# Block products of a two-level fast multiplication: the two whole ones also by quarters, one operand's sums streamed, another order

## The chip, the core and the metric

The kernel runs on one core of one Trainium2 chip. Time is device microseconds of one execution; it took 1370.39 us, the median of three (1369.78 to 1371.06). A core has TensorE (PE in the profile; PEld is its weight load), VectorE (DVE), ScalarE (ACT), GpSimd (POOL) and SyncE (SP), which here only issues DMAs. TensorE writes to PSUM, which holds eight banks of 512 float32 per partition; everything else lies in SBUF, 128 partitions wide.

## The reference, cut to what matters

```python
# q, k, v: (8, 8, 576, 64); tau = 0.02
scores = (1 / sqrt(64)) * (q @ k^T)
scores = where(scores >= max(scores) - tau, scores, -1e9)
attn   = exp(scores - max) / sum
x      = (attn @ v)  reshaped to (4608, 512)
g      = x @ w_gate                 # (512, 1536)
val    = x @ w_val                  # (512, 1536)
out    = (g * sigmoid(g) * val) @ w_out     # (1536, 512)
```

All of it is float32.

## The kernel before

**The work.** The eight batches are chunks 0 to 7 of 512 tokens; the last 64 tokens of each batch are gathered into a ninth, chunk 8 (`B` in the code). For every chunk the gate and value products are formed in six groups (`Group`, later `LateGroup`), and then the output product with w_out, which is what the change rewrites. The output product has an activation matrix of 512 tokens by 1536 and a weight matrix of 1536 by 512. From chunk 2 on (`DEEP = 2`) it is done in two levels of a seven-product scheme (Strassen's in Winograd's form). At the first level each matrix is cut into four blocks, and four blocks and three or four sums of blocks give seven pairs; a pair's product is called a step here. At the second level a step's two operands are cut in quarters again, so that the step itself is seven quarter products.

**The steps of a chunk** are methods of `Deep` (line 1433 on): p1 (operand 0), p2 (1), p3 (2), p4 (3), p5 (4), p6 (5), p7 (6). Steps by quarters call `nested` (line 1499): seven times three matmuls of 128x128 by 128x128, their matmul at line 1510. Steps p5 and p3 are whole: `flat` (line 1524) runs 2 x 6 matmuls with 256 columns, line 1519, with the tile name py. A nested step wants inner sums of its activation operand (`inner_sums`, line 1483: s3, s1, s2, s4, four additions of 128x384) and three sums of its weight operand. The weight sums are made once, on POOL during chunk 2, by `deepen` (line 1416): t1, t2, t4 go to a place in SBUF and t3 replaces a quarter of the operand. Five operands are treated so (`NESTED = 0, 1, 5, 6, 3`). A nested result is seven quarter products in two PSUM banks, and `combine` (line 1535) adds them up to an output block by four additions.

**Sums across steps.** p1's result is copied by ACT to SBUF (`copies`, line 1530), p2 is added in PSUM on top of it, combined and shipped; the copy is put back into PSUM by ACT (line 1625) so that p6 can be accumulated on it. p6's sum is copied out again, combined, and p3 on p5 is added; p7 is accumulated on the same bank and copied out, and p4 comes last on the same bank. `corner` (line 1681) adds p5's copy to the combined block.

**What sets the order.** The order of instructions is found when the program is built, by a planner (`Plan`, line 28): work on DVE, ACT, POOL and SP is given to it as jobs with an estimated duration, what they wait for and a rank (0 first), and it places them in time beside TensorE, whose order is written out. At run time each engine goes through its list in this order, waiting on semaphores. While attention of batches 1 to 7 runs (`halved`, 28 head pairs with three score groups each, line 1770), the feed-forward work of the earlier chunk is drawn from `sequence` (line 2007) between the score groups, so many steps a group as the tables say (`EARLY`, `SECOND`, `THIRD`, `MAIN`). `POOLED`, `EXCHANGE` and `CUTS` say for each score group how many of its tiles POOL scales and which engines exchange maxima and form thresholds. `attend` (line 1888, matmul xa at line 1904) multiplies the finished probabilities, which DVE has transposed (line 1883), with v.

**The tail.** After the last attend `tail[0]` is true, and chunks 7 and 8 run with nothing between their steps; the sums, which POOL does before, are then DVE's. A chunk's order of steps is

```python
# chunks 2 to 6
p1_first, last_gates, p1_rest, p2, p5, p6, p3, p7, p4
# chunk 7                     # chunk 8
p1, gates_end, p2, p7_alone,  p1, gates_end, p2, p7_alone,
p5, p6_alone, p3, p4_alone    p5_end, p6_alone, p4_alone, p3_end
```

**Weights of the next groups.** `flow` has two slots of seven 512-column parts for the gate and value weights. `load_flow` (line 949) loads a slot in two DMAs (1 MB and 0.75 MB). During the output steps the slots also hold activation sums (`s2`, `s3`, `place`), so a load is issued only after the step that reads these (`next_flow`, line 1731).

## Time and profile before

| what | us |
|---|---|
| median of three executions (1369.78 to 1371.06) | 1370.39 |
| the profiled execution | 1370.31 |
| its span in the profile | 1368.2 |
| DVE / ACT / POOL busy | 1090.6 / 866.7 / 714.2 |
| period of a middle chunk (p1_rest at 519.8, 666.4, 813.2, 959.8, 1106.5) | 146.6 |

Line numbers (L1510) are those of the kernel before; a group of instructions is named by line, engine, operation and out<-in tiles. A matmul of float32 leaves two records, so counts on TensorE are twice the number of matmuls. A timeline line gives start, duration, engine, line, operation and shape; what stands in brackets is how long the engine had been idle before it, and who ended that. The granted clock of TensorE was 0.997 of full speed.

### The profile page before, as it was taken

The numbers are of one execution on the slowest core, as the hardware profiler recorded it, in microseconds if no ns is written. First come the engines' busy times: TensorE is split into PE (matmuls) and PEld (weight loads), VectorE is DVE, ScalarE is ACT, GpSimd is POOL, SyncE is SP. The second block draws the span as 40 slices with busy tenths as digits, with TensorE's granted clock in tenths as the row PEclk, the third lists the DMA queues.
The fourth block names the chain that finished last, engine by engine and source line by source line (L and its number), as shares of the span: only waits on it lengthen the run. The fifth ranks groups of instructions, "written<-read, shape, count | busy, mean of one in ns | idle before, by whom it ended". The sixth has DMA issues, their size and how long they took to land.

```text
span 1368.2 us, 39123 instructions
## 1 busy us (share of the span) xinstructions
PE 1348.9 (99%) x15590; PEld 1126.1 (82%) x15590; DVE 1090.6 (80%) x2860; ACT 866.7 (63%) x2218; POOL 714.2 (52%) x664
## 2 busy tenths in 40 slices
PE   9999999999999999999999999999999999999998
PEld 7777887777788788878887788888887788999888
DVE  6788998888877778887878877887888776797786
ACT  6788765767765767677767676677767674330330
POOL 2688698754655669434972487437843592000000
PEclk9999999999999999999999999999999999999999
DMA  8752414466425440654154514543255404423411
GB/s 173 184 204 71 102 37 137 115 184 174 120 52 157 135 105 27 193 153 113 37 171 129 160 25 135 157 142 68 69 161 145 111 27 155 150 78 139 162 54 32
DMA packets 208293, 162.31 MB, mean 119 GB/s; under 512 B 166128, under 2 KB 180464, under 8 KB 202736
## 3 DMA queue, kind: packets, MB, share of 16 engines
q1 hardware_dynamic: 203920, 158.86, 41.2%
q8 instruction: 123, 2.02, 0.6%
q10 hardware_dynamic: 4192, 0.95, 0.3%
q14 instruction: 58, 0.48, 0.1%
HBM read 138.28 MB, written 21.50 MB: 117 GB/s over the span
## 4 chain that ended last, share of the span: by engine, by line
PE 89%; DVE 4%; POOL 2%; DMA 1%; issue 1%; SPq 1%; ACT 1%; ACTq 0%; DVEq 0%; POOLq 0%
PE pb L1021 17%; PE pa L1021 12%; PE px L1510 12%; PE sc L1770 10%; PE pe L1021 9%; PE xa L1904 9%; PE po L1303 5%; PE py L1519 5%; PE pg L1234 1%; PE sc L1188 1%; PE pv L1234 1%; PE pe L1188 1%; PE sc L1021 1%; POOL pall L495 1%; SPq L391 1%
## 5 line engine op out<-in xcount | busy, mean ns | idle before, releaser
L1846 ACT ACTIVATE pall<-sc,nm 128x288 f32<-128x288 f32 x504 | 234.2, 500 | 78.2 <-DVE pall L1848 42.5
L1848 DVE SCALAR_TENSOR_TENSOR pall<-sc,th,pall 128x288 f32<-128x288 f32 x504 | 243.7, 513 | 38.4 <-ACT pall L1846 21.9
L1021 PE MATMUL pb<-xall,big 128*128 128x256 f32 x1104 | 262.0, 380 | 0.0
L1021 PEld LDWEIGHTS pb<-xall,big 128*128 128x128 f32 x1104 | 207.5, 190 | 29.6 <-issue 1.6
L1883 DVE STREAM_TRANSPOSE pall<-pall 128x576 f32<-128x576 f32 x252 | 188.1, 764 | 28.9 <-POOL pall L1878 15.5
L1881 ACT ACTIVATE pall<-pall,ri 128x288 f32<-128x288 f32 x416 | 190.5, 526 | 22.8 <-DVE ri L1869 22.0
L1021 PE MATMUL pa<-xall,big 128*128 128x256 f32 x752 | 178.9, 381 | 0.3 <-ACT sc L1028 0.3
L1021 PEld LDWEIGHTS pa<-xall,big 128*128 128x128 f32 x752 | 140.7, 190 | 20.9 <-issue 2.5
L872 POOL TENSOR_TENSOR hall<-hall,tmp 128x512 f32<-128x512 f32 x80 | 102.5, 1281 | 104.9 <-DVE hall L1080 64.3
L1770 PE MATMUL sc<-kT,qT 64*32 64x288 f32 (+1 forms) x5376 | 145.5, 345 | 0.1
L1805 DVE TENSOR_REDUCE mx<-sc 128x2 f32<-128x576 f32 x168 | 118.4, 746 | 34.0 <-PE sc L1770 33.1
L1878 POOL TENSOR_SCALAR pall<-pall,ri 128x288 f32<-128x288 f32 x88 | 87.9, 1006 | 104.4 <-DVE ri L1869 75.4
L1021 PE MATMUL pe<-xall,big 128*128 128x256 f32 x576 | 138.4, 383 | 0.9 <-ACT pall L1881 0.9
L1770 PEld LDWEIGHTS sc<-kT,qT 64*32 64x32 f32 x5376 | 98.2, 106 | 49.9 <-issue 10.6
L1904 PE MATMUL xa<-pall,vall 64*32 64x288 f32 x4032 | 129.6, 404 | 3.0 <-PE px L1510 2.7
L1021 PEld LDWEIGHTS pe<-xall,big 128*128 128x128 f32 x576 | 107.6, 190 | 19.7 <-issue 4.3
L1904 PEld LDWEIGHTS xa<-pall,vall 64*32 64x32 f32 x4032 | 83.3, 107 | 42.0 <-issue 5.0
L872 POOL TENSOR_TENSOR tmp<-tmp 128x512 f32<-128x512 f32 x36 | 45.8, 1273 | 84.9 <-ACT tmp L1102 84.9
L1863 ACT COPY sums<-sums 32x6 f32<-32x6 f32 x336 | 66.6, 198 | 28.0 <-DVE pall L1848 23.9
L1079 ACT ACTIVATE vall<-tmp 128x512 f32<-128x512 f32 x96 | 60.0, 628 | 34.0 <-DVE tmp L1092 27.2
L1519 PE MATMUL py<-wo,hall 128*128 128x256 f32 x336 | 74.8, 379 | 0.0
L872 POOL TENSOR_TENSOR hall<-hall 128x384 f32<-128x384 f32 (+2 forms) x67 | 67.4, 1018 | 8.9 <-PE px L1510 8.2
(272 smaller groups left out, 2509.2 us busy)
## 6 DMA issues: line engine op xcount, KB each, us to landing
big<-sums_hbm SPq DMA_DIRECT2D x42, 1024.0 KB, 5.2
big<-sums_hbm SPq DMA_DIRECT2D x48, 768.0 KB, 4.6
vall<-in_v_dram SPq DMA_DIRECT2D x112, 144.0 KB, 3.1
out_dram<-big SPq DMA_DIRECT2D x32, 256.0 KB, 3.1
qT<-in_q_dram SPq DMA_DIRECT2D x112, 72.0 KB, 4.7
kT<-in_k_dram SPq DMA_DIRECT2D x112, 72.0 KB, 3.0
wo<-in_moe_w_gate_dram SPq DMA_DIRECT2D x16, 384.0 KB, 3.8
wo<-in_moe_w_val_dram SPq DMA_DIRECT2D x16, 384.0 KB, 4.7
```

The costliest lines, as they stand in the source:

```text
L872: return lambda: nc.gpsimd.tensor_tensor(out=out, in0=a, in1=b, op=op)
L1021: nc.tensor.matmul(ps[:, i], w[:, k_, i * P:(i + 1) * P], x[:, k_, :], start=first and i == k_ == 0, stop=True, skip_group_check=True)
L1510: nc.tensor.matmul(ps, a[:, f, :], ws[n][:, f, :], start=bank_ not in begun, stop=True, skip_group_check=True)
L1519: nc.tensor.matmul(ps(), a[:, f, i * P:(i + 1) * P], operands[o][:, f, :], start=first and f == 0, stop=True, skip_group_check=True)
L1770: nc.tensor.matmul(to[g * G:(g + 1) * G], qT[hs, col:col + G], kT[hs, c * SH + lo:c * SH + hi], start=True, stop=True)
L1805: rs.append(job("DVE", 0.72 if w > 1 else 0.42, lambda h=h: nc.vector.tensor_reduce(out=mx[:, n0 + h:n1 + h + 1:max(2, n1 - n0), 0], in_=s ...
L1846: ej = job("ACT", 0.44, lambda x=x, n=n: nc.scalar.activation(ps[x], scs[x], AF.Exp, bias=nm[:, n:n + 1]), ej, rank=top, on=on[x])
L1848: masks[x] = job("DVE", 0.48, lambda x=x, n=n: nc.vector.scalar_tensor_tensor(out=ps[x], in0=scs[x], scalar=th[:, n:n + 1], in1=ps[x], op0 ...
L1878: scaled.append(job("POOL", 1.02, lambda x=x, n=n: nc.gpsimd.tensor_scalar(out=x, in0=x, scalar1=ri[:, n:n + 1], scalar2=None, op0=ALU.mul ...
L1881: scaled.append(job("ACT", 0.46, lambda x=x, n=n: nc.scalar.activation(x, x, AF.Copy, scale=ri[:, n:n + 1]), rj, rank=rank))
L1883: seg["turned"].append(job("DVE", 0.72, lambda both=both: nc.vector.transpose(out=both, in_=both), *scaled, rank=rank))
L1904: nc.tensor.matmul(holds[a].ap()[x * G:(x + 1) * G, 0:SH].rearrange("d (i q) -> d i q", q=G), vr[rs, h, j, ds], p[rs, h, :, j, :], start=( ...
```

## The change

- Steps p5 and p3 become nested steps like the others, except the very last product, p3 of chunk 8 (`p3_end`), which stays whole. `flat` and `p5_end` go; `flat_half` stays for `p3_end`.
- Operands 4 and 2 get weight sums too, so seven are deepened. Those of operand 4 lie in spare places of SBUF. Those of operand 2 are stored in DRAM (`deep_hbm`) and loaded in each chunk to places that are free just then (`fetch_streamed`, two DMAs of 0.4 and 0.2 MB). Since p3 of chunk 8 reads the operand itself, the quarter that t3 replaced is saved too and loaded again after chunk 7 (`restore`).
- `inner_sums(4)` is added behind p1 and `inner_sums(2)` behind p7; each is four additions of 128x384. In the tail the inner sums of operands 2 and 3 are POOL's.
- The order of the steps is p7, p2, p5, p6, p4, p3 after p1 (in chunk 6 p3 before p4; in the tail p7, p2, p6, p5, p4, p3). p7 and p5 get pairs of banks of their own. p7's copy and p6's bank are added by DVE, and ACT copies this sum back to PSUM for p4 to be accumulated on. `corner` adds p5's copy to that sum (896 columns) and then combines.
- `next_flow` calls move: slot 0's second part behind p7, slot 0's first behind p6, slot 1's second behind p5, and slot 1's first behind p3 (behind p6 before).
- `s_place` moves to `pall`, and the tables of steps, pooled scales, exchanges and cuts have other values.

```diff
@@ -1406,5 +1406,17 @@
+    SPARE_SUMS, STREAMED = 4, 2
+    loose = whole[:, SPARE + P + NF2 * TC:SPARE + P + NF2 * TC + 2 * QW]
+    ends = vends.rearrange("p a n -> p (a n)")[:, 0:QW]
+    streamed = tmp.rearrange("p a f n -> p (a f n)")[:, 2 * NQ * P:2 * NQ * P + 2 * QW], flow[:, GW + 3 * HW:GW + 3 * HW + QW]
+    deep_stored = []
     def deeper_part(o, n):
-        lo = (3 * NESTED.index(o) + n) * QW
-        return deeper[:, lo:lo + QW].rearrange("p (f q) -> p f q", q=P)
+        if o in (SPARE_SUMS, STREAMED):
+            two, one = (loose, ends) if o == SPARE_SUMS else streamed
+            place = two[:, n * QW:(n + 1) * QW] if n < 2 else one
+        else:
+            lo = (3 * NESTED.index(o) + n) * QW
+            place = deeper[:, lo:lo + QW]
+        return place.rearrange("p (f q) -> p f q", q=P)
@@ -1417,3 +1429,4 @@
         b11, b12, b21, b22 = quarters(operands[o])
-        t1, t2, t4 = (deeper_part(o, n) for n in range(3))
+        t1, t2, t4 = (deeper_part(o, n) if o != STREAMED else free_place[:, n * QW:(n + 1) * QW].rearrange("p (f q) -> p f q", q=P)
+                      for n in range(3))
         j = job("POOL", 1.0, pool_tt(t1, b12, b11, ALU.subtract), *deps, rank=3)
@@ -1421,3 +1434,23 @@
         j = job("POOL", 1.0, pool_tt(t4, b21, t2, ALU.subtract), j, rank=3)
-        deep_jobs[o] = [job("POOL", 1.0, pool_tt(b12, b22, b12, ALU.subtract), j, rank=3)]
+        kept = None
+        if o == STREAMED:
+            deep_stored.append(job("SP", 0.1, lambda: nc.sync.dma_start(out=deep_hbm[:, 0:3 * QW], in_=free_place[:, 0:3 * QW]), j, lag=2.0, moves=2.2))
+            kept = job("SP", 0.3, lambda: nc.sync.dma_start(out=deep_hbm[:, 3 * QW:].rearrange("p (f q) -> p f q", q=P), in_=b12), *deps,
+                       lag=2.0, moves=0.8)
+            deep_stored.append(kept)
+        deep_jobs[o] = [job("POOL", 1.0, pool_tt(b12, b22, b12, ALU.subtract), j, kept, rank=3)]
+    def fetch_streamed(*deps):
+        two, one = streamed
+        def fn():
+            nc.sync.dma_start(out=two, in_=deep_hbm[:, 0:2 * QW])
+            nc.sync.dma_start(out=one, in_=deep_hbm[:, 2 * QW:3 * QW])
+        return job("SP", 0.2, fn, *deep_stored, *deps, lag=1.6, moves=2.2)
+    def restore(*deps):
+        b12 = quarters(operands[STREAMED])[1]
+        deep_jobs[STREAMED] = [job("SP", 0.3, lambda: nc.sync.dma_start(
+            out=b12, in_=deep_hbm[:, 3 * QW:].rearrange("p (f q) -> p f q", q=P)), *deps, lag=2.0, moves=0.8)]
...
@@ -1436,3 +1469,3 @@
         def __init__(self, c, mark):
-            self.c = c
+            self.c, self.at_end = c, tail[0]
             halves = [hall[:, t].rearrange("p g f n -> p (g f) n") for t in range(2)]
@@ -1442,2 +1475,3 @@
             self.place = flow[:, 0:KW]
+            self.late_place = flow[:, GW + 4 * HW:GW + 4 * HW + KW]
             assert GW - KW >= 4 * HW
@@ -1446,10 +1480,13 @@
             self.blocks = 0
+            self.c5 = self.u2 = None
             if tail[0]:
-                self.steps = deque([self.p1, self.gates_end, self.p2, self.p7_alone, self.p5, self.p6_alone, self.p3, self.p4_alone])
-                self.spaces = [pall[:, n * CW:(n + 1) * CW] for n in range(5)]
+                self.steps = deque([self.p1, self.gates_end, self.p7_alone, self.p2, self.p6_alone, self.p5, self.p4_alone, self.p3])
+                self.spaces = [*(pall[:, n * CW:(n + 1) * CW] for n in range(4)), w_second[:, 0:CW]]
                 if c == B:
-                    self.steps = deque([self.p1, self.gates_end, self.p2, self.p7_alone, self.p5_end, self.p6_alone, self.p4_alone, self.p3_end])
+                    self.steps = deque([self.p1, self.gates_end, self.p7_alone, self.p2, self.p6_alone, self.p5, self.p4_alone, self.p3_end])
             else:
-                self.steps = deque([self.p1_first, self.last_gates, self.p1_rest, self.p2, self.p5, self.p6, self.p3, self.p7, self.p4])
-                self.spaces = [*spaces, None, spaces[1]]
+                self.steps = deque([self.p1_first, self.last_gates, self.p1_rest, self.p7, self.p2, self.p5, self.p6, self.p4, self.p3])
+                if c == B - 2:
+                    self.steps = deque([self.p1_first, self.last_gates, self.p1_rest, self.p7, self.p2, self.p5, self.p6, self.p3, self.p4])
+                self.spaces = [*spaces, None, spaces[0]]
             self.ready["a11"] = [gated[c, 0, x] for x in range(NF2 // 2)]
@@ -1462,3 +1499,3 @@
             self.ready["s1"] = [self.sum(self.a21, self.a21, self.a22, ALU.add, x, j3[x], gated[c, 1, n + x]) for x in range(n - 1)]
-            self.inner_sums(6, self.s3, free_place, j3)
+            self.inner_sums(6, self.s3, free_place, j3, *deep_stored)
@@ -1476,2 +1513,5 @@
             self.inner_sums(5, self.s2, self.place, self.ready["s2"], self.m1)
+            self.inner_sums(4, self.a21, self.late_place, self.ready["s1"], mark)
+            if self.c < B:
+                self.fetched = fetch_streamed(*u_list[3].jobs, *s_list[0].jobs, mark)
@@ -1487,4 +1527,4 @@
             s1, s2, s3, s4 = (flat[:, n * QW:(n + 1) * QW].rearrange("p (f q) -> p f q", q=P) for n in range(4))
-            tt, eng, took = (dve_tt, "DVE", 0.49) if tail[0] else (pool_tt, "POOL", 1.0)
-            rank = 1 if o in (1, 5) else 2
+            tt, eng, took = (dve_tt, "DVE", 0.49) if self.at_end and o not in (2, 3) else (pool_tt, "POOL", 1.0)
+            rank = 1 if o in ((1, 4, 5) if self.at_end else (1, 4, 5)) else 2
             j3 = job(eng, took, tt(s3, a11, a21, ALU.subtract), *ready, *deps, rank=rank)
...
@@ -1628,18 +1662,22 @@
             self.ready["s4"] = s4
+            if self.c == B - 2:
+                self.last_sums(self.m7)
             self.inner_sums(3, self.a22, self.a11, self.ready["a22"], m)
+            if self.c < B and self.c != B - 2:
+                self.last_sums(self.m7)
         def p5(self):
-            self.y = y = take("py")
-            m = self.flat(4, self.a21, y, True, *y.deps, *self.ready["s1"])
-            t = self.spaces[4]
-            self.c5 = job("ACT", 0.57, lambda: nc.scalar.copy(t[:, 0:DM], y.ap()), m, *u_list[1].jobs, *u_list[2].jobs, *u_list[3].jobs, rank=0)
...
+            self.y, deps = self.pair("py")
+            m = self.nested(4, self.y, True, *deps)
+            self.c5 = self.copies(self.spaces[4], self.y, m, *(() if self.at_end else self.z))
+            self.next_flow(1, 1, m)
+            if not self.at_end:
+                self.try_corner()
+                return
+            t, j = self.spaces, self.u3
+            if self.c == B:
+                self.done(self.y, *self.c5)
+                j = job("DVE", 1.05, dve_tt(t[2], t[2], t[4], ALU.add), j, *self.c5, rank=1)
+                self.n12, self.j12 = self.combine(t[2], j)
+            self.corner(t[3], j)
@@ -1647,4 +1685,5 @@
             o = self.block(self.n12).rearrange("p (i n) -> p i n", i=2)
-            for i, y in enumerate(self.ys):
-                m = self.flat_half(2, self.a12, i, lambda y=y: y.ap()[:, 0:DM2], False, self.c5[i], *self.ready["s4"])
+            for i in range(2):
+                y = take("py")
+                m = self.flat_half(2, self.a12, i, lambda y=y: y.ap()[:, 0:DM2], True, *y.deps, *self.ready["s4"], *deep_jobs[2])
                 j = job("DVE", 0.4, lambda i=i, y=y: nc.vector.tensor_tensor(out=o[:, i], in0=y.ap()[:, 0:DM2], in1=o[:, i], op=ALU.add),
@@ -1657,30 +1696,47 @@
             m = self.nested(5, self.x, False, *self.z)
+            x, t = self.x, self.spaces
             self.next_flow(0, 0, m)
-            self.next_flow(1, 0, m, *self.ready["s4"])
-            self.c6 = self.copies(self.spaces[2], self.x, m, *n_list[0].jobs, *n_list[1].jobs)
-            self.n12, self.j12 = self.combine(self.spaces[2], *self.c6)
+            self.c6 = self.copies(t[2], x, m, *n_list[0].jobs, *n_list[1].jobs)
+            a, b = x
+            js = [job("DVE", 0.7, lambda: nc.vector.tensor_tensor(out=t[1][:, 0:4 * P], in0=a.ap(), in1=t[1][:, 0:4 * P], op=ALU.add),
+                      m, *self.c7, rank=0),
+                  job("DVE", 0.56, lambda: nc.vector.tensor_tensor(out=t[1][:, 4 * P:CW], in0=b.ap()[:, 0:3 * P], in1=t[1][:, 4 * P:CW],
+                                                                   op=ALU.add), m, *self.c7, rank=0)]
+            self.u2 = js[1]
+            self.try_corner()
+            self.z2 = [job("ACT", 0.57, lambda: nc.scalar.copy(a.ap(), t[1][:, 0:4 * P]), js[0], self.c6[0], rank=0),
+                       job("ACT", 0.46, lambda: nc.scalar.copy(b.ap()[:, 0:3 * P], t[1][:, 4 * P:CW]), js[1], self.c6[1], rank=0)]
         def p3(self):
-            y = self.y
-            m = self.flat(2, self.a12, y, False, self.c5, *self.ready["s4"])
-            o = self.block(self.n12)
-            j = job("DVE", 0.7, lambda: nc.vector.tensor_tensor(out=o, in0=y.ap(), in1=o, op=ALU.add), m, self.j12, rank=0)
-            y.read_by(j)
-            y.done(True)
-            self.ship(0, 1, self.n12, j)
+            t = self.spaces[2]
+            m = self.nested(2, self.y, False, *self.c5, self.fetched)
+            n, j = self.combine(t, *self.add(t, self.y, t, m, *self.c6, self.u3 if self.at_end else None))
+            self.ship(0, 1, n, j)
             for b in n_list:
                 b.jobs = [*b.jobs, j]
-            self.next_flow(1, 1, m)
+            for b in (u_list[3], s_list[0]):
+                b.jobs = [*b.jobs, m]
+            self.next_flow(1, 0, m)
+            if self.at_end:
+                restore(m)
         def p7(self):
-            m = self.nested(6, self.x, False, *self.c6)
-            self.next_flow(0, 1, m)
-            self.c7 = self.copies(self.spaces[0], self.x, m, *self.z)
-            self.corner(self.spaces[0], *self.c7)
+            y, deps = self.pair("py")
+            m = self.nested(6, y, True, *deps)
+            self.next_flow(0, 1, m, *self.ready["s2"])
+            self.c7 = self.copies(self.spaces[1], y, m, *u_list[1].jobs, *u_list[2].jobs, *u_list[3].jobs)
+            self.done(y, *self.c7)
+            self.m7 = m
+        def try_corner(self):
+            if self.c5 and self.u2:
+                self.corner(self.spaces[1], self.u2)
+        def last_sums(self, *deps):
+            self.inner_sums(2, self.a12, free_place, self.ready["s4"], *deps)
         def corner(self, t, *deps):
-            n, j = self.combine(t, *deps)
-            o, s = self.block(n), self.spaces[4][:, 0:DM]
-            tt, eng, took = (dve_tt, "DVE", 0.62) if tail[0] else (pool_tt, "POOL", 1.3)
-            j = job(eng, took, tt(o, o, s, ALU.add), j, *(self.c5 if self.c == B else [self.c5]), rank=1)
+            s = self.spaces[4]
+            tt, eng, took = (dve_tt, "DVE", 1.05) if tail[0] else (pool_tt, "POOL", 2.1)
+            n, j = self.combine(s, job(eng, took, tt(s, s, t, ALU.add), *deps, *self.c5, rank=1))
             self.ship(1, 1, n, j)
@@ -1688,5 +1744,7 @@
                 b.jobs = [*b.jobs, j]
+            if self.at_end:
+                w_users[1] = [j]
         def p4(self):
-            m = self.nested(3, self.x, False, *self.c7)
+            m = self.nested(3, self.x, False, *self.z2)
             n, j = self.combine(self.x, m, psum=True)
@@ -1708,7 +1766,4 @@
             self.next_flow(0, 0, m)
-            self.next_flow(1, 0, m, *self.ready["s4"])
             self.next_flow(0, 1, self.m7)
-            self.n12, self.j12 = self.combine(t[2], *self.c6)
-            self.u3 = job("DVE", 1.05, dve_tt(t[3], t[2], t[3], ALU.add), *self.c6, *self.c7, rank=1)
-            self.corner(t[3], self.u3)
+            self.u3 = j = job("DVE", 1.05, dve_tt(t[3], t[2], t[3], ALU.add), *self.c6, *self.c7, rank=1)
@@ -2032,10 +2087,10 @@
     EARLY = (2, 2, 3, 1, 2, 3, 1, 3, 4, 1, 3, 3)
-    SECOND = (2, 5, 7, 3, 6, 5, 3, 6, 5, 3, 4, 4)
-    THIRD = (2, 5, 8, 3, 5, 7, 4, 7, 7, 1, 2, 2)
-    MAIN = (1, 3, 8, 3, 5, 7, 4, 7, 7, 1, 2, 2)
-    LATE = (0, 1, 4)
-    LATE_SECOND = (0, 2, 4)
-    POOLED = (2, 1, 1, 0, 2, 1, 1, 0, 0, 0, 1, 1)
-    EXCHANGE = ('BOTH', 'DVE', 'BOTH', 'ACT', 'BOTH', 'DVE', 'DVE', 'ACT', 'ACT', 'BOTH', 'ACT', 'BOTH')
-    CUTS = ('ACT', 'DVE', 'ACT', 'DVE', 'DVE', 'ACT', 'ACT', 'DVE', 'DVE', 'DVE', 'ACT', 'DVE')
+    SECOND = (2, 5, 7, 3, 6, 5, 3, 6, 5, 5, 3, 5)
+    THIRD = (2, 5, 6, 5, 5, 7, 2, 7, 4, 4, 2, 2)
+    MAIN = (2, 4, 6, 3, 6, 7, 3, 7, 7, 1, 2, 2)
+    LATE = (2, 3, 4)
+    LATE_SECOND = (1, 2, 3, 4)
+    POOLED = (1, 3, 0, 2, 1, 1, 0, 0, 0, 0, 0, 0)
+    EXCHANGE = ('ACT', 'BOTH', 'ACT', 'ACT', 'DVE', 'DVE', 'ACT', 'DVE', 'DVE', 'BOTH', 'BOTH', 'BOTH')
+    CUTS = ('DVE', 'DVE', 'ACT', 'DVE', 'ACT', 'DVE', 'DVE', 'ACT', 'DVE', 'DVE', 'DVE', 'DVE')
```

31 lines of the change are left out of this document (11 added, 20 removed).

## The prediction

> **What bounds the kernel now.** I read the share of each engine first, then the chain of work that ended last, the waits of TensorE, and then the timelines of the stretches that the change rewrites.
>
> ```profile
> span 1368.2 us, 39123 instructions
> ## 1 busy us (share of the span) xinstructions
> PE 1348.9 (99%) x15590; PEld 1126.1 (82%) x15590; DVE 1090.6 (80%) x2860; ACT 866.7 (63%) x2218; POOL 714.2 (52%) x664
> ```
>
> TensorE is busy for 99% of the span, and the waits that its view of waits lists come to 15 us, 9 of them in the first attention stage (lines 265 to 531). So the time is TensorE's own work, plus whatever new waits the change makes. The chain in the output stage of chunk 3 (one of seven two-level chunks, 2 to 8; the middle ones repeat every 146.6 us), columns start, duration, what:
>
> ```profile
> 666.41 3.56 PE px L1510 x30
> 669.97 0.53 issue
> 670.49 4.70 PE xa L1904 x144
> 675.19 1.47 PE sc L1770 x58
> 676.66 4.88 PE px L1510 x42
> 681.54 5.18 PE py L1519 x24
> 686.72 1.65 PE sc L1770 x64
> 688.37 4.88 PE px L1510 x42
> 693.25 5.18 PE py L1519 x24
> ```
>
> A px piece of 42 records is one block product by quarters (7 x 3 matmuls of 128 columns, two records each); a py piece of 24 is one whole product (12 matmuls of 256 columns). After a score group (sc) the px piece takes 4.88. In the tail, with no scores between, the two stand side by side:
>
> ```profile
> 1237.54 5.18 PE py L1519 x24
> 1242.72 4.69 PE px L1510 x42
> ```
>
> **Removed: TensorE work.** Steps p5 and p3 (operands 4 and 2) of chunks 2 to 8 are the 14 whole products; 13 become quarter products (the last one of chunk 8 stays whole). The instruction order confirms it: 156 fewer 128x256 and 273 more 128x128 matmuls. Each saves 5.18 - 4.69 = 0.49 us: 13 x 0.49 = **-6.4 us**, on the path. The number of score and attend runs stays 85, so the 0.19 of a first piece after scores is not changed. The Trainium skill (TensorE: Matmul & The Clock Gate, section "Wait — 56ns, not 53.3ns?") puts a fixed 2.5 ns on every matmul beside its columns; from its figures, with two passes a record, a record of this quarter product is an estimated 109 ns and the saving 7.7 us; a record of the whole product comes out at 216 ns, as in the trace (5.18/24). The rows give 4.69/42 = 112 ns, and the sum goes by them.
>
> **Moved: the order of softmax work.** Five times attend waits half a microsecond:
>
> ```profile
> PE xa L1904 <- PE px L1510: 2.7, 5, 0.5
> ```
>
> The real releaser is DVE's last transpose of the probabilities, since attend depends on it and it ends at 670.39 just before attend starts at 670.49:
>
> ```profile
> 666.47 1.42 DVE L1805 TENSOR_REDUCE mx<-sc 128x2 f32<-128x576 f32 x2 [0.18 <-PE sc L1770]
> ...
> 669.61 0.78 DVE L1883 STREAM_TRANSPOSE pall<-pall 128x576 f32<-128x576 f32 x1
> ```
>
> In chunks 3 to 6 the new tables put that transpose and the last gate product ahead of the score maxima. ACT's last scaled tile (666.85) then lets it end near 667.9, two microseconds before attend can start. The gain lies between 0 (the delayed maxima make the next score group late instead) and 5 x 0.53 = 2.7; I take 4 x 0.53 = **-2.1 us**.
>
> **Added: waits at p4.** The old order put p3 or an attend between a copy and the product that reads it. Now p6 is followed in chunks 2 to 5 by one score group (1.65) and then by p4, which needs ACT's new copies of the summed block back to PSUM. Behind p6's end ACT has 0.17 to start, 0.58 + 0.48 for the old pair of copies (rows at 693.35 and 694.43 show 0.59 and 0.47) and 0.58 for the first new one: 1.8, and 0.1 to reach TensorE. That is 1.9 against 1.65: 0.25 late. DVE's two new PSUM additions (0.69 and 0.55, as in the tail) run beside it.
>
> The other input of p4 is POOL's. POOL's order in such a chunk runs without a gap from the last gate product to the last inner sum of p4: 8 sums of 128x512 at 1.24 pitch, 19 of 128x384 at 1.0, 4 token sums at 0.72, one query scaling at 1.7, and the new 128x896 addition at 1.28 x 896/512 = 2.2. Sum 35.7 us. The 384 price is from
>
> ```profile
> L872 POOL TENSOR_TENSOR hall<-hall 128x384 f32<-128x384 f32 x40 | 39.7, 1001 | 8.9 <-PE px L1510 8.2
> ```
>
> If the gate product starts at 667.25 (last gates end 664.76; the DVE product now at 666.5 for 0.69), POOL is done at 702.95. TensorE reaches p4 at 669.97 + 6.17 + 4.88 + 4.69 + 1.65 + 4.88 + 4.69 + 1.65 = 698.6 and needs that sum for its last seventh, 0.19 + 4.0 later, at 702.8, plus the 0.25 above. So the two meet within 0.2. I cost 0.4 a chunk, 4 x 0.4 = **+1.6 us**, between 0.25 (1.0) and 2.1 a chunk (8.4, below). In chunk 6 p3 stands ahead of p4 and an attend between them; nothing is charged.
>
> **Added: the tail of chunk 7.** In the tail all sums were DVE's, and POOL was idle from 1139.5 on. Now the inner sums of p4 and p3 go to POOL, 8 operations in chunk 7 and 4 in chunk 8. The only place in this trace where DVE operations with two SBUF inputs meet POOL is the weight stage:
>
> ```profile
> 89.82 0.94 DVE L348 SCALAR_TENSOR_TENSOR big<-wo,big 128x768 uint32<-128x768 uint32 x1
> 96.71 2.88 DVE L348 SCALAR_TENSOR_TENSOR big<-wo,big 128x768 uint32<-128x768 uint32 x2
> ```
>
> ```profile
> 96.64 1.27 POOL L611 TENSOR_TENSOR hall<-hall,tmp 128x512 f32<-128x512 f32 x1
> ```
>
> Two of 0.94 took 2.88 while POOL held 96.64 to 97.91: DVE stood for 1.0 until POOL had ended. By this row the sums exclude each other. In chunk 7, in old times, p2 now ends at 1237.55 and p6 follows. POOL starts the four inner sums of p4 there. DVE adds four PSUM pieces until 1239.7 and has six SBUF sums left, two of which p6 needs for its last two sevenths. Alternating with POOL's third and fourth sum (1.0 each), those two land at 1243.05 and 1244.4; p6 asks for them at 1240.9 and one seventh later: 2.25 + 0.65 = **+2.9 us**. Without exclusion they land at 1241.0 and 1242.3, which costs 0.8. I take 2.9. Chunk 8 has no such meeting: without eight token sums, DVE is done with p6's inputs before p2 ends.
>
> The Trainium skill (SBUF — State Buffer, section "SBUF: two separate sides") calls the port pair that DVE and GpSimd share an exclusive lock for the whole instruction. It speaks against this move, and the row agrees; that float32 sums do the same is shown by no row of before.
>
> **At nothing.** The streamed operand: two loads (0.4 and 0.2 MB) per chunk, issued behind p1, read by p3 some 30 us later, against 5.2 us for a 1 MB load; if that cover goes, p3 waits for the rest. The first half of the next chunk's second weight slot is now loaded after p3 instead of p6, some 18 us before its reader in the middle chunks and 10 in the tail (against 5.2); queued behind it on SP are only loads with later readers. Eight more POOL operations build the two new operands in chunk 2, where POOL has gaps of 3 to 7 us. For small waits of scheduling that I do not see, **-0.1 to +1**, taken as 0. The last store still leaves after the last whole product, so the 3.7 us behind TensorE stay.
>
> Sum: -6.4 - 2.1 + 1.6 + 2.9 = -4.0. The profiled execution took 1370.31 us (span 1368.2 and 2.1 around it), 0.08 under the median 1370.39, so the forecast is **1366.3 us**.
>
> **Rivals.**
> - The saving is eaten (24%): attend's wait stays or moves to the next score group, and p4 waits 1.0 a chunk: -6.4 + 4.0 + 2.9 = +0.5, 1370.8. For it: DVE's maxima really move back by 1.4 us. Against: the score group reuses banks that are freed in turn.
> - POOL becomes the bound at p4 (13%, slower): one chain of 35.7 us without slack, four times. If the gate product starts at 668.8 as it did before (1.6 late) and chained sums take 1.03 (4.13 for four in the old timeline, 0.5 over 16 of them), p4 waits 2.1: 8.4 instead of 1.6, and attend's gain goes with it, since the same late DVE causes both: -6.4 + 8.4 + 2.9 = +4.9, 1375.2. It makes the kernel slower than can be overlooked once p4 waits 1.6 a chunk.
> - It goes better (18%): no exclusion in the tail and all of attend's wait gone: -6.4 - 2.7 + 1.2 + 0.8 = -7.1, 1363.2.
> - That the products are not replaced is excluded by the instruction order.
>
> **Chances and range.** The forecast, 1364 to 1367.6, has 45%. A measurement of this kernel can tell about 0.2%, 2.7 us. Faster by more: 45 + 18 = 63%; within it 24%; slower 13%. The range leaves out most of the slower rival and the end of the better one: 1362.5 to 1371.8. The likeliest side's own range is 1362.5 to 1367.6.
>
> **What would show it.** One py piece of 24 records is left, all other products are pieces of 42 at 4.7 to 4.9; attend's five waits vanish; the waits of TensorE of the px products in chunks 2 to 5 name ACT or POOL at p4 and stay under half a microsecond; in chunk 7 p6 shows a DVE wait of two to three, with DVE sums of 0.5 stretched to 1.5 beside POOL. Wrong would be p4 waits above 1.5, a wait of p3 for the streamed load, or new waits at the score groups.

## The result: slower, and where the time appears

The changed kernel takes 1409.81 us, the median of five (1405.56 to 1412.54), beside 1371.06 of the kernel before (five, 1369.78 to 1373.25): a ratio of 1.0274, 95% interval 1.0248 to 1.0301. The forecast was 1366.3. The profiled execution took 1405.66.

The first lines of its page; the columns are as in the page of before:

```profile
span 1403.9 us, 39744 instructions
...
PE 1359.2 (97%) x15824; PEld 1134.6 (81%) x15824; DVE 1135.2 (81%) x2896; ACT 879.9 (63%) x2224; POOL 770.2 (55%) x715
```

TensorE is busy 10.3 us longer, though its products became shorter, and idle for the rest of the 35.7 by which the span grew. Its waits (total, times, longest):

```profile
PE sc L1825 <- DVE pall L1903: 11.5, 5, 4.8
PE sc L1825 <- DMA qT<-in_q_dram: 5.7, 1, 5.7
...
PE xa L1959 <- issue: 4.3, 1, 4.3
...
PE px L1550 <- DVE big L876: 1.9, 2, 1.6
...
PE px L1550 <- ACT px L1707: 0.7, 1, 0.7
PE xa L1959 <- PE px L1550: 0.7, 1, 0.7
```

The score groups (sc) wait for VectorE's masks (line 1903, 1848 before), which they did not do before; new waits there are one of the signs of being wrong that the prediction names. The 5.7 put down to a DMA has the same cause: masks stand ahead of the last query transpose in VectorE's list. Attend's wait of five halves of a microsecond is down to one, as forecast. VectorE's list behind the first of these waits (start, duration), in chunk 2:

```profile
549.69 0.12 DVE L1891 TENSOR_REDUCE nm<-mx 128x6 f32<-128x12 f32 x1
549.85 6.71 DVE L1895 TENSOR_SCALAR th<-nm,cut 128x6 f32<-128x6 f32 x1
556.48 0.77 DVE L1938 STREAM_TRANSPOSE pall<-pall 128x576 f32<-128x576 f32 x1
```

The threshold, six numbers a partition, takes 6.71 us; the median of its 62 is 0.36. In the kernel before none of the thresholds takes over 1.02 (duration ns min/median/max):

```profile
L1840 DVE TENSOR_SCALAR th<-nm,cut x52: 221/241/1019, 150.0 to 1132.0; 128x6 f32<-128x6 f32 x52
```

GpSimd at the time of the 6.71:

```profile
548.05 3.72 POOL L873 TENSOR_TENSOR hall<-hall,big 128x512 f32<-128x512 f32 x3
551.72 1.01 POOL L873 TENSOR_TENSOR hall<-hall 128x384 f32<-128x384 f32 x1
...
555.53 1.00 POOL L873 TENSOR_TENSOR hall<-hall 128x384 f32<-128x384 f32 x1
```

Its last sum ends at 556.53, and the threshold at 556.56. The same happens in chunks 4, 5 and 6 (6.95, 6.93 and 7.13 us, each ending 0.03 behind GpSimd's run), not in chunk 3 (1.21). By the times between attends, chunks 2, 4 and 5 are 153 to 156 us long and chunk 3 is 147; chunk 6 has no such time, since attention ends in it. Four pauses of TensorE of 4.3 to 5.7 us follow (at 561, 863, 1018 and 1179). In the four stretches of 50 us that hold them TensorE's granted clock is 0.93, in the four ahead of these 1.00. Two of them (bounds; length; busy PE, PEld, DVE, ACT, POOL with their instructions; clock, DMA share, GB/s):

```profile
800.00:850.00 50.00, 50.00 (x650) 42.57 (x642) 40.46 (x116) 37.13 (x95) 42.53 (x41) 1.00 0.25 64
850.00:900.00 50.00, 44.98 (x559) 37.84 (x558) 41.45 (x97) 29.49 (x81) 29.37 (x31) 0.93 0.45 128
```

The score group that follows the pause of 4.8 us, at 863.21, takes 3.57 where others take 1.72.

### The profile page after: what moved, and what is told of

It is laid out like the page before. It is cut to its first block, busy times and chain, and to the rows that moved or that the text cites. A ratio compares the mean times of both kernels' runs of the same rounds, so it can differ in the third digit from the quotient of the medians.

```text
span 1403.9 us, 39744 instructions
## 1 busy us (share of the span) xinstructions
PE 1359.2 (97%) x15824; PEld 1134.6 (81%) x15824; DVE 1135.2 (81%) x2896; ACT 879.9 (63%) x2224; POOL 770.2 (55%) x715
## 4 chain that ended last, share of the span: by engine, by line
PE 82%; DVE 9%; DMA 2%; issue 2%; POOL 2%; ACT 2%; SPq 1%; DVEq 0%; ACTq 0%; POOLq 0%
PE pb L1022 18%; PE pa L1022 12%; PE sc L1825 9%; PE xa L1959 9%; PE pe L1022 9%; PE px L1550 8%; PE po L1303 5%; PE py L1550 5%; DVE th L1895 2%; PE pe L1188 1%; PE sc L1188 1%; DVE pall L1903 1%; PE sc L463 1%; DVE mx L1860 1%; SPq L392 1%
## 5 line engine op out<-in xcount | busy, mean ns | idle before, releaser
L1022 PE MATMUL pb<-xall,big 128*128 128x256 f32 x1152 | 274.7, 381 | 0.0
L1022 PEld LDWEIGHTS pb<-xall,big 128*128 128x128 f32 x1152 | 215.7, 190 | 32.5 <-ACT vall L1080 2.7
L1936 ACT ACTIVATE pall<-pall,ri 128x288 f32<-128x288 f32 x426 | 195.6, 525 | 27.8 <-DVE ri L1924 26.7
L1022 PE MATMUL pa<-xall,big 128*128 128x256 f32 x768 | 182.6, 381 | 0.0
L873 POOL TENSOR_TENSOR hall<-hall 128x384 f32<-128x384 f32 (+2 forms) x75 | 78.8, 1066 | 184.6 <-PE sc L1550 184.3
L1825 PE MATMUL sc<-kT,qT 64*32 64x144 f32 (+1 forms) x5376 | 156.2, 353 | 20.0 <-DVE pall L1903 11.5
L1825 PEld LDWEIGHTS sc<-kT,qT 64*32 64x32 f32 x5376 | 101.7, 108 | 75.1 <-DVE pall L1903 19.4
L1933 POOL TENSOR_SCALAR pall<-pall,ri 128x288 f32<-128x288 f32 x78 | 77.8, 1007 | 101.6 <-DVE ri L1924 63.3
L873 POOL TENSOR_TENSOR tmp<-tmp 128x512 f32<-128x512 f32 (+1 forms) x41 | 56.3, 1374 | 59.0 <-DVE tot L1923 29.6
L873 POOL TENSOR_TENSOR big<-hall 128x384 f32<-128x384 f32 (+2 forms) x71 | 67.6, 966 | 33.9 <-PE pa L1022 26.3
```

Source lines behind the costliest of these rows:

```text
L873: return lambda: nc.gpsimd.tensor_tensor(out=out, in0=a, in1=b, op=op)
L1022: nc.tensor.matmul(ps[:, i], w[:, k_, i * P:(i + 1) * P], x[:, k_, :], start=first and i == k_ == 0, stop=True, skip_group_check=True)
L1825: nc.tensor.matmul(to[g * G:(g + 1) * G], qT[hs, col:col + G], kT[hs, c * SH + lo:c * SH + hi], start=True, stop=True)
L1933: scaled.append(job("POOL", 1.02, lambda x=x, n=n: nc.gpsimd.tensor_scalar(out=x, in0=x, scalar1=ri[:, n:n + 1], scalar2=None, op0=ALU.mul ...
L1936: scaled.append(job("ACT", 0.46, lambda x=x, n=n: nc.scalar.activation(x, x, AF.Copy, scale=ri[:, n:n + 1]), rj, rank=rank))
```

## The experiments

The theory at first: a threshold on VectorE is held up while GpSimd strings sums together that do not depend on each other. The main rival: the other added work costs the time. Kernels are called by the number in front of their label.

**The threshold on ScalarE (e1).**

```diff
-    CUTS = (..., 'DVE', 'DVE', 'DVE', 'DVE')
+    CUTS = (..., 'DVE', 'DVE', 'DVE', 'ACT')
```

> The changed kernel with one word changed: the threshold (th<-nm,cut) of the last score group of each cycle, drawn just before p5, is made by ScalarE, as it is for two other groups of the table, and not by VectorE. Theory A (VectorE's threshold of 0.36 us is held up for as long as GpSimd strings independent sums together, 6.7 to 7.1 us in chunks 2, 4, 5 and 6; masks, the next scores and the granted clock follow): the four long thresholds vanish, the PE waits that name VectorE's masks (11.5 us in 5) fall below 3 us, the chunk periods of 153.4 to 156.2 us fall to about 147, and the time to 1366 to 1373 us. Theory B (the time goes to the rest of the change: the longer ScalarE and GpSimd chains around p4, the streamed operand's transfers, the retuned shares of work): the periods stay at 153 or more and the time at 1400 to 1410 us. If another VectorE operation is held up in the threshold's place, the time lands between the two.

1379.41 us (ten runs), ratio 1.0074 [1.0056, 1.0092]. By the ratios the changed kernel lost 2.7% of the time before, some 38 us; 2.0%, some 27 us, hang on this one operation of 0.36. The span is 1374.6, which is 29.3 less: 12.7 of busy TensorE (1346.5; an estimate from the clock, 4 x 50 us x 0.07 = 14, is near it) and 16.6 of waiting. The periods fall to 146.7 and 148. The theory's time was too low: some 10 us above the kernel before remain, where 4 below it was forecast.

**Dependent copies behind the inner sums (e2).** In `inner_sums` for p3 and p4: `nc.gpsimd.tensor_copy(spacer, out[:, 2, P - 1:P])` after each sum on GpSimd.

> The changed kernel with the threshold left on VectorE; behind each of the eight GpSimd inner sums of p3 and p4 in a chunk a one-column GpSimd copy is added that reads the sum's last column, so that every second GpSimd instruction depends on the one before it. GpSimd does more work than before this edit (8 short copies a chunk), in the same order, and no other engine's instructions change. Theory A (it is the unbroken run of independent instructions that holds VectorE's threshold up): the threshold gets in at the first such dependence, 3.5 us at most where the three s4 sums are still running and below 2.5 otherwise, and the time falls to 1366 to 1378 us. Theory A' (GpSimd's being busy is enough, whatever the instructions depend on): the threshold waits for the whole, now longer run, 7.5 us or more, and the time is 1405 us or above. Theory B (the rest of the change): 1400 to 1412 us with short thresholds or long ones.

1385.92 us, 1.0107 [1.0079, 1.0136]. The thresholds take 2.91 in chunk 2 and 2.17 to 2.19 in chunks 3 to 5, and 0.47 in chunk 6: each held one ends 0.03 behind the first sum with a dependent copy. GpSimd does more, and the kernel is faster than the changed one by 1.7% of the time before; its being busy is not the cause.

**Before, with three sums made again (e4, e5).** In e4 (shown) s3 is made again behind each of the other three sums of p3; in e5 those three are made again behind the last, so that most sums depend on the one before.

```diff
-            j1 = job(eng, took, tt(s1, a21, a22, ALU.add), ...)
+            j1 = job(eng, took, lambda: (t1(), again and t3()), ...)   # j2, j4 too
```

> The kernel before, in which GpSimd's four inner sums of p3 become seven: the first one (s3, the same values to the same place) is made again behind each of the other three, so that no sum reads what the one just before it wrote. Nothing else changes on any engine. Theory A: the threshold that starts about 1 us into this run and took 1.02 us now waits for the run's end, some 5 to 6 us in most of the chunks 2 to 6, and the time rises by 3 to 9 us for each such chunk, to 1385 to 1410 us. Theory A' (GpSimd's being busy is enough): the same here, and the same in the twin kernel with dependent repeats. Theory B (the change's other parts cost the time): 1370 to 1373 us, since 3 us more on an engine busy for less than half of the span hide.

> The twin of the one before it: the kernel before with seven inner sums of p3 in the place of four on GpSimd, but the three repeats are the second, third and fourth sum again (same values, same places), in an order in which five of the seven read or follow what the one just before them wrote, so that no more than two independent sums stand together. GpSimd's work is that of the twin. Theory A: the threshold gets in after 2.1 us at most, and the time stays at 1370 to 1374 us. Theory A': the threshold waits 5 us or more and the time rises as in the twin. Theory B: 1370 to 1373 us in both.

1376.01 us, 1.0048 [1.0031, 1.0065], and 1377.87, 1.0058 [1.0042, 1.0074]. In the output stages no threshold takes over 1.02 us in either (e5 has one of 1.66 in the stage that makes the weights' sums): seven separate sums do not hold it up. **This falls against the theory as it stood.** By the times between attends the kernels lose 1.7 to 2.6 (e4) and 2.2 to 3.1 us a chunk (e5) in another way: attend waits 1.3 (e5: 1.8) four times, behind a tile that GpSimd scales after these sums. Three microseconds more on an engine that is busy 52% of the span were not free.

**The lock by itself (e6).** GpSimd runs of eight, and one VectorE operation in each.

> A kernel that leaves the whole computation out and measures the disputed cost by itself: 130 sections, in each of which GpSimd makes eight operations of 128x384 f32 (none; eight sums that do not read each other; two interleaved chains; one chain; eight scalings with one SBUF operand), and one VectorE operation becomes ready about 0.5 us behind the first of them. The VectorE operations: the threshold's form (128x6, a scalar read from SBUF), the same with immediates, the threshold's form 384 wide, sums of two SBUF operands (384 and 6 wide), a sum with a PSUM operand, the masks' form with a PSUM operand, a transpose, a maximum, a reciprocal. Theory A: beside eight separate sums and beside interleaved chains the threshold's form takes most of the 7.7 us of the run, in the single chain 1 to 2 us, and alone 0.1 to 0.3; of the others those that took their usual time beside GpSimd in the kernel (transpose, maximum, masks, sums with PSUM) are not held up. Theory A' (busy is enough): the single chain holds it up as long as the others do. Theory B needs none of them to be held up for more than one GpSimd operation, 1 us.

No run holds anything for longer than to the next boundary of two GpSimd sums. Beside GpSimd sums (alone in brackets): threshold's form 0.47 (0.23), with immediates 0.47 (0.17), 384 wide 0.66 (0.42), sum of two SBUF operands 0.85 (0.56), of 6 columns 0.46 (0.17). Not delayed: a sum with a PSUM operand 0.56, the masks' form 0.62, transpose 0.58, maximum 0.16, reciprocal 0.19. GpSimd's scalings with one SBUF operand delay nothing. That is why masks and transposes never showed it. Theory A falls in this form.

**Runs and moments (e7).**

> A kernel that leaves the whole computation out: 115 sections, five kinds of GpSimd run by 23 moments at which VectorE's threshold (128x6, right behind a small minimum, as in the kernel) becomes ready, 0.3 to 1.4 us behind the run's start in steps of about 0.05. The runs: eight sums that do not read each other; the changed kernel's own run (three in-place sums of 128x512, then the four inner sums of p3 and of p4 by turns); the run of the kernel before (three in-place sums, then one chain of four); the two chains by turns alone, written to two tiles, and to one. In the measurement of the lock by itself, where the moment never varied, the threshold got in at the next boundary of two GpSimd sums in all runs. Theory A2 (it usually gets in at the next boundary, but a threshold that misses its boundary because of its moment or because of the operands misses the following ones too, until GpSimd pauses or an instruction depends on the one just before it): in the two kinds of alternating runs, or at some moments, the threshold takes 3 to 10 us, and never more than 2.2 in the run with one chain. Theory A3 (nothing in GpSimd's run itself holds it off, and it needs what only the whole kernel has, such as work of the other engines): no threshold above 1.6 us in any kind.

In each of the two alternating kinds 7 of 23 thresholds are held, for 7.5 to 8.5 us, to the end of the run; in the other three kinds none takes over 1.34. The same boundary of the same run lets one in and holds another, at all moments, so neither moment nor operands decide. In these two kinds alone GpSimd went from one run into the next without a pause. The traces of the kernels show what their held thresholds share: GpSimd had then worked for 14.2 to 15.0 us without a gap. A gap here is also the short one of a dependence: a sum that reads what the one before it wrote starts 0.07 us behind the latter's end, a separate one a few hundredths of a microsecond ahead of it. At the thresholds of the output stages of the kernel before, GpSimd had so worked for 5.3 us at most. The held threshold and chunk 3's free one can have the same age (14.94 us in chunks 3 and 4, with the same instructions around them), so near this age one and the same stretch can do either.

**Age or count (e8).**

> A kernel that leaves the whole computation out. In each of 33 sections GpSimd makes forty sums of 128x384 f32 without a pause (about 38 us), and VectorE, which waits for nothing, makes transposes (0.5 us each, not held up in the earlier measurements) with thresholds between them: the first one 0.5, 4, 8, 14 or 20 us behind the run's start, the others every 1.8 to 10 us. Three kinds of run: separate sums, two chains by turns, and separate sums with a one-column copy that depends on the fourth, eighth, ... of them. So far every held-up threshold stood in a GpSimd stretch without a gap of more than 14 us that had already let one threshold in. Theory C (the count decides): the first threshold of a section gets in at the next boundary, 0.25 to 1.2 us, however late it comes, and the second or the third is held up to the end of the run, tens of us. Theory D (the time decides): the thresholds of the first 10 us all get in, and any that comes 14 us or more behind the run's start is held up to the end, also as the first of its section. Under both, no threshold takes over 5 us in the kind with dependent copies. If all of them get in within 1.2 us, neither holds.

Thresholds of one section of separate sums, in GpSimd's run of 38.09 us that starts at 60.23, and the first of another, whose run starts at 357.79:

```profile
60.56 0.69 DVE L58 TENSOR_SCALAR e<-nm,ptr 128x6 f32<-128x6 f32 x1
64.72 0.34 DVE L58 TENSOR_SCALAR e<-nm,ptr 128x6 f32<-128x6 f32 x1
...
72.35 0.34 DVE L58 TENSOR_SCALAR e<-nm,ptr 128x6 f32<-128x6 f32 x1
76.16 22.20 DVE L58 TENSOR_SCALAR e<-nm,ptr 128x6 f32<-128x6 f32 x1
...
373.45 22.46 DVE L58 TENSOR_SCALAR e<-nm,ptr 128x6 f32<-128x6 f32 x1
```

Up to 12.1 us into the run they get in; the one at 15.9 is held to the end. The last row is a first request, and is held as well. In the two kinds without dependent copies, of 50 thresholds up to 13.1 us into the run none is held (1.04 at most). Of 15 at 15.7 us or later, with none let in during the last 7 us, 14 are held. Of 26 at 14.1 us or later that follow another by less than 4 us, one is. With a dependent copy every fourth sum none of 58 is held, at any age (0.97 at most). So age decides (theory D), with one thing added: a threshold let in shortly before keeps the door open. That the sums are separate matters, as far as these runs show, because nothing then ends the stretch; the dependent copies start 0.06 us behind their sums here. Whether a copy ends the stretch because it depends on a sum, or because it is another kind of operation than a sum, no run separates; the query scaling inside the stretch of chunk 2 (546.36 to 548.09) did not end it.

The Trainium skill (SBUF — State Buffer, section "SBUF: two separate sides") lets whichever starts first have the shared pair for the whole instruction. The runs agree for young stretches; 22.20 us is 23 GpSimd instructions, and that page has no such case.

**The stretch broken in the kernel (e12).** A dependent copy behind each of the three s4 sums, threshold on VectorE.

> The changed kernel, threshold on VectorE, with a one-column GpSimd copy behind each of the three s4 sums of a chunk that depends on the sum (three short copies a chunk, all other engines' instructions as they are). In the kernel the held-up thresholds come 14.2 to 15.0 us into a GpSimd stretch without a gap, during or just before these sums. Theory D (a threshold is let in at every boundary where the stretch is young or an instruction depends on the one before it): none of the last groups' thresholds takes over 2.5 us and the time is that of the run with the threshold on ScalarE, 1376 to 1383 us. If the copies do not help, 1400 us or more.

1381.58 us, 1.0078 [1.0059, 1.0097]. The row of its thresholds, behind that of the changed kernel (duration ns min/median/max):

```profile
L1895 DVE TENSOR_SCALAR th<-nm,cut x62: 214/358/7128, 151.0 to 1160.3; 128x6 f32<-128x6 f32 x62
```

```profile
L1895 DVE TENSOR_SCALAR th<-nm,cut x62: 215/356/1685, 151.5 to 1141.1; 128x6 f32<-128x6 f32 x62
```

The 1685 stand in the stage of the weights' sums; in the output stages none takes over 1.18. Three copies a chunk do what moving the threshold does, within the intervals. Theory D stands in the kernel.

**The tail undone (e3).** `if self.at_end and o not in (2, 3)` becomes `if self.at_end`, on top of e1.

> The changed kernel with the threshold of the last score group on ScalarE, and with the inner sums of the last two chunks' p3 and p4 on VectorE, as the kernel before had those of its p4, and not on GpSimd. It undoes the tail's term of the prediction too (2.9 us estimated by a row of sums that exclude each other, 0.8 without; 1.91 of waits at chunk 7's p6 measured in the changed kernel). Theory A with that term: 1.5 to 2.5 us below the run with the threshold alone moved, so 1364 to 1371 us, and below the kernel before. If the tail's waits only pass to the next product: the same time as that run within 0.5 us. Theory B: 1398 to 1408 us.

1378.26 us, 1.0056 [1.0040, 1.0073]: not told apart from e1. p6 of chunk 7 now waits 0.34 alone, but p4's last seventh waits 1.58 for VectorE's longer list: the wait has passed to a later product.

**Where the other 10 us are (e9, e10, e11).** The edits: `range(NF2)` becomes `range(NF2 - i)` in the whole products of before; the p3 sums are not issued (on e1); the query scaling is a ScalarE activation (on e1).

> The kernel before, without the last of the twelve matmuls of each whole product (a part of the sum over the hidden dimension is left out): its 14 whole products become 0.43 us shorter, nearly the 0.49 that a product by quarters saves, and no other instruction changes. Theory E (in the output stage the softmax work of a score group, not TensorE, sets the pace, and what a product saves is waited for at the next score group): the time falls by less than half of 14 x 0.43 = 6.0 us, to 1366 to 1371 us. Theory F (the stage has slack in the old order, and the change lost its gain by its own moves and additions): the time falls by 5 to 6 us, to 1362.5 to 1365.5 us beside a kernel before of 1368 to 1371.

> The changed kernel with the threshold on ScalarE, without GpSimd's inner sums of operand 2's product p3, four operations of 1 us a chunk (p3 then multiplies what lies in their places, so that its part of the output is left out). No other instruction changes. The repeated sums in the kernel before cost 1.6 to 2.2 us a chunk with nothing else changed. Theory G (GpSimd has no 3 us to spare in the output stage: its longer chain delays the query scaling and with it VectorE's transposes and the next scores): the score groups lose their waits, and the time falls by 6 to 10 us against the run with the threshold alone moved, to 1369 to 1373 us. Theory E (the softmax work of VectorE and ScalarE): the time falls by less than 2 us.

> The changed kernel with the threshold on ScalarE and with the query scaling (1.7 us of GpSimd for every pair of heads, in the output stage and elsewhere) on ScalarE (an estimated 0.8 us: 0.45 for 288 columns there, by two). The planner sets the other engines' order anew by this. Theory G: GpSimd's chain gets 1.7 us shorter where it is late and the queries come earlier: 1368 to 1374 us. Theory E: ScalarE, with more to do in the same stage, is later with the masks' exponentials: the same as the run with the threshold alone moved, or slower, 1379 to 1385 us.

e9: 1364.69 us, 0.9956 [0.9940, 0.9971], which is 6.0 us (4.0 to 8.2), as much as the products became shorter. Theory E falls: in the old order a shorter product pays in full. e10: 1.0044 [1.0025, 1.0063], not told apart from e1, with periods of 146.7 and 148.8 beside e1's 146.7 and 148.0; theory G is not borne out. e11: 1.0111 [1.0090, 1.0132], slower than e1: the score groups wait 5.4 for masks instead of 2.4.

**Order and shares (e13, e14).** p3 ahead of p4 in chunks 2 to 5; the tables of before, with only the last threshold on ScalarE.

> The changed kernel with the threshold on ScalarE, and with p3 ahead of p4 in chunks 2 to 5 too, as chunk 6 has them (GpSimd's inner sums in that order as well). What p4 waits for (ScalarE's copies back of the summed block, 0.75 a chunk, 3.0 us in all) then has a whole product more time. If p4's wait is simply cover that the change took away: 3 us less, 1374 to 1378 us. If the attend that waits 2.7 us in chunk 6 is the price of that order, it appears in the other chunks too: +2.7 x 4 - 3.0 = +8, 1385 to 1390 us.

> The changed kernel with the tables that share out the work (steps drawn per score group, GpSimd's part of the scaling, who exchanges maxima, who makes the thresholds) those of the kernel before, and the threshold of the last group on ScalarE. Only the products, their sums and their order are then new. Theory H (the products and their sums are worth what the forecast says, and the new tables cost the rest): 1366 to 1372 us. Theory I (the tables were fitted to the new products, which cost it without them): 1382 us or more. In between: both have a part.

e13: 1386.76 us, 1.0107 [1.0076, 1.0137]. p4's wait is gone, and the time rises, but not by attend's 2.7, which stays single; a gate product waits 2.2, one product 1.2 for GpSimd's sums, and the score groups 6.8 where e1's wait 4.8. e14: 1413.51 us, 1.0312 [1.0289, 1.0335]. There p4 waits 8.0 us in four for GpSimd's inner sums and attends 16.9 in ten. So the forecast's slower rival, which put 2.1 a chunk at p4, describes what the old shares do: 2.25 at p4's last seventh in three of these chunks.

**The added work left out (e16, e17, e18),** all on e1.

> The changed kernel with the threshold on ScalarE, without any GpSimd inner sum of the two products that are newly made by quarters (p5 and p3, eight operations of 1 us a chunk; these products multiply what lies in the sums' places, so that their parts of the output are left out). No other instruction changes. Theory G (GpSimd's added work is what the score groups wait for): 1366 to 1372 us, 7 to 12 us below the run with the threshold alone moved. Theory J (the new copies and additions on ScalarE and VectorE, and the order that goes with them): 1375 to 1380 us.

> The changed kernel with the threshold on ScalarE, without VectorE's two additions in PSUM's place (L1701 and L1703) and ScalarE's two copies back (L1707 and L1708) of each of chunks 2 to 6, so that a part of each output is left out. No other instruction changes. Theory J: p4's wait of 0.75 a chunk goes, and with it a part of the score groups' waits: 1370 to 1376 us. Theory G: only p4's 3.0 us go: 1375 to 1378 us.

> Both at once: without GpSimd's eight new inner sums a chunk and without the additions and copies back. What stays of the change are its products, their order and the retuned shares of work. If the added work is what the change lost, this is the forecast without its added terms, -6.4 - 2.1 = -8.5 against the kernel before, 1361 to 1366 us. If it stays above 1370 us, the order and the shares themselves cost the rest.

e16: 1.0071 [1.0046, 1.0097], as e1, though eight GpSimd sums a chunk are gone: theory G falls. e17: 1.0039 [1.0018, 1.0061], about 5 us less than e1; e1's waits at p4, which this edit removes, are 3.0. e18: 1375.22 us, 1.0035 [1.0023, 1.0048], 4.8 above the kernel before, where the forecast without its added terms is 8.5 below. GpSimd still made p4's sums, so that the tail's wait of 2.6 is in it. That leaves 11 us or so to what e18 keeps of the change, its order and its shares above all. This is by exclusion: the streamed operand, the moved loads of weights and the copies of p7 and p5 are kept too, though no wait of TensorE in e1 or e18 names a load of the streamed operand.

Part of them can be read. The waits of e1, and VectorE's list ahead of its attend at 1149.61:

```profile
PE px L1550 <- ACT px L1707: 3.0, 4, 0.8
PE xa L1959 <- issue: 2.7, 1, 2.7
PE sc L1825 <- issue: 2.4, 4, 0.9
PE sc L1825 <- DVE pall L1903: 2.4, 3, 1.3
```

```profile
1147.71 0.65 DVE L1779 TENSOR_TENSOR vall<-py,vall 128x512 f32<-128x512 f32 x1
1148.29 0.54 DVE L1781 TENSOR_TENSOR vall<-py,vall 128x384 f32<-128x384 f32 x1
1148.76 0.76 DVE L1938 STREAM_TRANSPOSE pall<-pall 128x576 f32<-128x576 f32 x1
```

The 2.7 are the last transpose, placed behind two additions that read the product just ended. The 2.4 of "issue" stand at the same four of TensorE's matmul records in e1, e16 and e18 (numbers 4639, 6664, 7550 and 10589 of its list) with lengths of 0.34 to 1.49. No semaphore explains them, but the DMA records hold a lead. The program itself is loaded in pieces of 16 KB on a queue named "instruction", 125 in e1, one for every 250 or so of TensorE's records (matmuls and weight loads). Each of these twelve waits ends 2.2 to 2.5 us behind the start of such a piece, and these pieces start late: 404 to 480 records behind the one before, where the median is 250 to 252. That TensorE waits there for its own instructions fits this; no run tests it.

## Why the prediction was wrong, point by point

**Shorter products, -6.4: right.** One py piece of 24 records is left, in chunk 8 (1394.59). In chunk 3 of e1 the two products between two score groups take 9.57, twice (from 680.08 and 691.30), where they took 10.06 (from 676.59 and 688.30), and e9 shows that such time reaches the end in the old order.

**Attend, -2.1: right where it was looked at, given back beside it.** Four of five waits are gone. But in e1 the score group behind that attend takes 1.96 instead of 1.73, and the second one behind the next attend 2.07 instead of 1.65: 0.65 a chunk. The timelines put this to the maxima and masks, which moved back, the cost that the first rival named; no run tests it alone. One attend lost 2.7 anew (4.3 with the held threshold).

**p4, +1.6: mechanism right, size off.** 0.75 a chunk and 3.0 in all, named ACT, not POOL. The working let ScalarE's copy-out run beside VectorE's addition from the same PSUM bank. In e1 it waits for it: the addition starts at 995.63, the copy at 996.36.

**Tail of chunk 7, +2.9: mechanism right, size off.** Sums of two SBUF operands do exclude each other in float32. GpSimd's four take 6.38, two of VectorE's are stretched, and p6 waits 1.57 and 0.34, 1.9 in all:

```profile
1272.92 6.38 POOL L873 TENSOR_TENSOR hall<-hall 128x384 f32<-128x384 f32 x4 [93.75 <-PE sc L1550]
```

```profile
1277.23 1.22 DVE L876 TENSOR_TENSOR kT<-xall,qT 128x256 f32<-128x256 f32 x1
1278.38 1.34 DVE L876 TENSOR_TENSOR big<-big 128x384 f32<-128x384 f32 x1
```

**"At nothing", -0.1 to +1: this is the step that failed.** Beyond p4 it priced eight more GpSimd sums a chunk and the new order at nothing. The prediction had both halves of the answer: it wrote that GpSimd's chain in such a chunk runs without a gap for 35.7 us, and that VectorE stood until GpSimd's sum had ended (line 348). It used the lock in the tail alone and never asked which VectorE operations inside that chain want the pair. The threshold does. In the kernel before it gets in at the next boundary of two sums (0.98 to 1.02 us); in the changed kernel's stretches, 14 us and more old by then, it gets in at none in four chunks of five. That is some 27 of the 38 us; e1, e2, e12 and e8 show it. No rival had it: the slower one put the price at p4, and its 1.6 a chunk was not reached.

**The rest, 14 us from -4 to +10.** p4 is 1.4 of it, and the tail gives 1.0 back. Most, some 11, lies by exclusion in the order and the shares (e18); the pieces read in e1 (2.7, 2.4, and 0.65 in each of five chunks) would make up 8 of them, and the others stay open. The cause of the 2.4 is open too. Moved work was priced only where it took a wait away.

## What to carry to other kernels

When work is added to GpSimd, list its stretches without a gap, not its share: an engine at 55% held stretches of over 20 us here. Then look in that stretch for the VectorE operations that e6 found delayed (thresholds, sums of two SBUF operands), small ones too, and move them to ScalarE, or break the stretch with a short copy that depends on the sum before it. And do not count on a saving on the critical engine at its full size when the order around it changes: it paid in full where the order stayed (e9), and not where it changed (e18).

## What the runs showed of the hardware that was not expected

A VectorE threshold (128x6, read from and written to SBUF) gets in between two GpSimd sums in the first 13 us of an unbroken stretch. From 15.7 us on, with none let in during the last 7, it is mostly held to the stretch's end (14 of 15), up to 22.5 us here. What in the chip ages is not shown: time and the number of instructions (0.95 us each) grow together in these runs. Nor is age the whole rule: chunk 3's threshold got in at 14.9 us (1.21), while that of chunk 4, at the same age, was held. In the stage that makes the weights' sums the threshold at 26 us gets in at the next boundary in both kernels (0.40 and 0.41), and is held until GpSimd's next gap in nine of the other kernels (1.66 to 1.70). A pause of about 5 us costs more than itself: in the changed kernel each of four came with a clock of 0.93 over 50 us, and 12.7 of the 29.3 us by which e1 is shorter were busy time.
